# Another order for the jobs of an attention and gated convolution kernel

## The chip, the cores and the metric

The kernel runs on one core of a Trainium2 chip. The metric is the time of one execution on the device in microseconds (us), as the median of several runs. The engines are TensorE (PE in the profile, PEld its weight loads), VectorE (DVE), ScalarE (ACT), GpSimd (POOL) and SyncE (SP, which here only starts DMAs).

## The reference

```python
def _attn_ref(q, k, v):                    # (8, 8, 576, 64) each, float32
    ...                                    # rotary embedding of q and k by position
    scores = scale * np.matmul(q_rot, k_rot.transpose(0, 1, 3, 2))
    scores = scores - np.max(scores, axis=-1, keepdims=True)
    attn = np.exp(scores)
    attn = attn / (np.sum(attn, axis=-1, keepdims=True) + 1e-09)
    return np.matmul(attn, v)

def _moe_ref(x, w_val, conv_w, w_out):     # x: the 8 heads side by side, (8, 576, 512)
    ...                                    # xp: x with 4 rows of zeros in front
    for k in range(5):
        gate_pre += conv_w[k] * xp[:, k:k + S, :]
    gate = 1.0 / (1.0 + np.exp(-gate_pre))
    return gate * (x @ w_val) @ w_out
```

The two weight matrices and the convolution's taps arrive as 64-bit floats and are decoded on the chip.

## The kernel before

**Tiling.** The 64 heads are worked on as 32 pairs (p = 0 to 31), four pairs to a batch. A pair's q and k lie as 128 partitions (two heads of 64) by 576 positions. For a pair: the rotation is two multiplications and one addition each for q and k (`rope_mul`, `rope_add`; pair 0 adds on TensorE, `rope_mm`, with a matrix `swap` that ACT makes). Scores (`s_mm`) are computed for four blocks of 128 query rows by 576 keys and head, and for a fifth half block of both heads together (`s_mm` and `s_mix`). DVE takes the row maximum while it copies the scores to SBUF (`s_max`, line 428), ACT the exponential and its row sum (`s_exp`, line 436). TensorE transposes the result (`t_mm`, line 412), ACT or DVE copies it (`t_copy`), and TensorE multiplies with v (`pv_mm`, line 518, in four jobs for a pair, and `pv_left`, line 528, for the last 64 keys). The reciprocals of the row sums go through DRAM to be spread over the partitions (`r_write`, `r_read`), and `x_norm` multiplies with them. For pairs 0 to 6 (`WHOLE`) q and k stay in full precision; from pair 7 on they are split into a high and a low part (`qk_hi`, `qk_lo`), and a score is three products.

**The gated part.** Each pair's normalised x is one of four channel blocks of its batch. It is split into high and low (`x_hi`, `x_lo`); five taps make the gate (`tap`, `gate`); once all four pairs of a batch are there, two projections follow (`f_mm`, line 636: stage 0 with w_val, stage 1 with w_out, eight parts for each of four outputs), with `y_mul`, `y_hi`, `y_lo` between them and `o_out`, `o_dma` at the end. The weights are decoded in eight steps for each of eight blocks (`weight_step`), the taps in six (`tap_step`), both early in the kernel.

**Order.** Nothing is scheduled by a planner at run time. Functions add 3087 jobs to a list, with the engines that may do each and what it reads and writes. `ORDER` then says in which order they are issued: an entry is a job's number; V, A or G behind it chooses DVE, ACT or POOL where several may do it; the digits after a colon choose the buffers of the rings that the job opens (for TensorE one of four PSUM units); `<` names a job that this one is to wait for in addition. Every engine, and SP's DMA queue, works through its own entries in this order and waits, at each, for what its inputs and buffers need. `FILLS` puts 20 transpositions of the identity ahead of one entry.

**Numbers that come up.** 0: load of the taps, 1 to 6 their decoding; 7 and 8: the table's halves (on ACT's queue); 9: `tab_wrap`; 10: `make_swap`; 11, 16: loads of k of pair 0, 22, 31: of q; 27, 28: rotation multiplications of q's columns 0 to 256, 23, 24: 256 to 384, 32, 33: 384 to 640; 12, 13 and 17, 18: of k's halves; 14, 19, 25, 29, 34: `rope_mm`; 37: the first score job, 38 its maximum; 99 to 107 and 108 to 116: load and eight decoding steps of two blocks of w_val; 142, 143 and 141: rotation of q of pair 1; 136 to 139: of k of pair 1, with its wrap; 386: the first projection job; 2950 and 2955: the two transpositions of the last pair's sums (`r_mm`, line 550), 2949 and 2954 their reciprocals (`r_inv`); 2669 to 2672: four projection jobs of batch 6; 2933: a transposition of the last pair and 2934 its copy; 3047 to 3085: the last batch's outputs.

## Time and profile before

| | |
|---|---|
| runs | 620.99 us median of 3 (620.88 to 621.19) |
| profiled execution | 620.63 us, its span 618.8 us |
| TensorE busy | 609.4 us (98%), 8797 matmuls |
| DVE, ACT, POOL busy | 526.8 us (85%), 472.9 us (76%), 328.6 us (53%) |
| chain that ended last | PE 88%, DVE 6%, DMA 2%, ACT 2% |

A page of the profile tells of one execution. Busy shares are means over stages. In the chain of waits each piece is what the next one had waited for; its share says where the time passed that could not be overlapped. An engine's idle time costs something only where it stands on that chain. TensorE's records of matmuls overlap, so that a busy TensorE may still pass fewer matmuls than it could. L428 means line 428 of the kernel.

### The profile page before, as it was taken

The page shows a single profiled execution, that of the slowest core. Times are in us where ns is not written, and L with a number is a line of the kernel's source. Part 1 is how long each engine was busy: PE and PEld are TensorE (multiplying, and loading weights), DVE is VectorE, ACT ScalarE, POOL GpSimd, SP SyncE. Part 2 cuts the span into 40 slices and gives each one's busy share as a digit, 9 for nine tenths or more (in the row PEclk, how much of TensorE's full clock was granted, in tenths as well). Part 3 has the DMA queues.
Part 4 walks back from the last instruction along what each step waited for, and adds up shares of the span by engine and source line. Part 5 has one row for each costly group of instructions (what it writes and reads, how often), then busy time and mean ns, then how long its engine had stood idle before and what let it go on. Part 6 is the DMA issues. An engine that isn't in the chain of part 4 may idle for free.

```text
span 618.8 us, 21223 instructions
## 1 busy us (share of the span) xinstructions
PE 609.4 (98%) x8797; PEld 511.8 (83%) x8797; DVE 526.8 (85%) x1091; ACT 472.9 (76%) x993; POOL 328.6 (53%) x306
## 2 busy tenths in 40 slices
PE   8899999999999999999999999999999999999997
PEld 7566679888897979879898889788888889889697
DVE  6999999999998899998888888989888888777653
ACT  4999999999878887788887788766768775767421
POOL 2366444635445656466455457564454654688441
PEclk9999999999999999999999999999999999999999
DMA  8564631543524341435343234342333524201202
GB/s 252 171 200 149 197 115 58 155 138 119 158 68 147 100 137 64 139 118 158 117 140 119 81 119 137 116 140 64 96 119 100 177 62 149 90 20 52 71 21 77
DMA packets 42722, 72.85 MB, mean 118 GB/s; under 512 B 15449, under 2 KB 18050, under 8 KB 42626
## 3 DMA queue, kind: packets, MB, share of 16 engines
q1 hardware_dynamic: 41938, 70.74, 36.3%
q8 instruction: 69, 1.13, 0.8%
q10 hardware_dynamic: 688, 0.75, 0.4%
q14 instruction: 27, 0.22, 0.1%
HBM read 61.89 MB, written 9.59 MB: 115 GB/s over the span
## 4 chain that ended last, share of the span: by engine, by line
PE 88%; DVE 6%; DMA 2%; ACT 2%; issue 1%; SPq 0%; DVEq 0%; POOL 0%; POOLq 0%
PE ps_f L636 34%; PE ps_a L518 18%; PE ps_s L392 16%; PE ps_t L412 11%; PE ps_s L402 4%; PE ps_a L528 3%; DVE p L428 3%; ACT p L436 1%; ACT pt L505 1%; PE ps_s L412 1%; DMA wst<-in_w_val 1%; DVE qin L312 1%; DMA rb<-rd 1%; DMA tab<-in_tab 1%; DVE pm L428 0%
## 5 line engine op out<-in xcount | busy, mean ns | idle before, releaser
L436 ACT ACTIVATE p<-p,nm 128x576 f32<-128x576 f32 x256 | 197.3, 773 | 33.3 <-DVE p L428 32.1
L428 DVE TENSOR_SCALAR_CACHE_REDUCE p<-ps_s 128x576 f32<-128x576 f32 x256 | 184.1, 752 | 24.3 <-PE ps_s L392 21.4
L505 ACT COPY pt<-ps_t 128x1024 f32<-128x1024 f32 (+1 forms) x138 | 126.0, 929 | 23.8 <-PE ps_t L412 22.3
L392 PE MATMUL ps_s<-k,q 64*128 64x288 f32 x1424 | 137.5, 316 | 1.6 <-DVE q L318 0.5
L518 PE MATMUL ps_a<-pt,v 128*64 128x320 f32 (+1 forms) x1024 | 133.2, 410 | 0.1
L392 PEld LDWEIGHTS ps_s<-k,q 64*128 64x128 f32 x1424 | 111.5, 185 | 17.6 <-issue 4.0
L636 PE MATMUL ps_f<-y,wout_hi 64*128 64x288 f32 (+2 forms) x1024 | 109.0, 298 | 0.0
L518 PEld LDWEIGHTS ps_a<-pt,v 128*64 128x64 f32 x1024 | 69.9, 137 | 47.1 <-DVE p L428 1.1
L606 DVE SCALAR_TENSOR_TENSOR g<-x,cw,g 128x576 f32<-128x576 f32 (+2 forms) x113 | 93.3, 828 | 7.1 <-POOL g L604 3.6
L412 PEld LDWEIGHTS ps_t<-ident,p 64*128 64x128 f32 x2172 | 86.1, 139 | 10.3 <-issue 2.2
L412 PE MATMUL ps_t<-ident,p 64*128 64x64 f32 x2172 | 92.2, 223 | 0.4
L636 PEld LDWEIGHTS ps_f<-y,wout_hi 64*128 64x128 f32 x1024 | 87.1, 186 | 0.6 <-DVE x L577 0.2
L636 PE MATMUL ps_f<-xh,wval_hi 64*128 64x288 f32 (+2 forms) x512 | 84.8, 303 | 0.0
L636 PE MATMUL ps_f<-xl,wval_hi 64*128 64x288 f32 (+2 forms) x512 | 82.0, 292 | 0.0
L636 PE MATMUL ps_f<-xh,wval_lo 64*128 64x288 f32 (+2 forms) x512 | 82.0, 292 | 0.0
L636 PE MATMUL ps_f<-y,wout_lo 64*128 64x288 f32 (+2 forms) x512 | 81.7, 292 | 0.0
L312 POOL TENSOR_TENSOR kin<-kin,tab 128x576 f32<-128x576 f32 x41 | 58.3, 1428 | 37.5 <-DVE q L352 12.5
L312 POOL TENSOR_TENSOR qin<-qin,tab 128x640 f32<-128x640 f32 x32 | 50.0, 1566 | 36.1 <-DVE g L606 10.4
L636 PEld LDWEIGHTS ps_f<-xh,wval_hi 64*128 64x128 f32 x512 | 54.6, 185 | 0.8 <-issue 0.5
L636 PEld LDWEIGHTS ps_f<-xl,wval_hi 64*128 64x128 f32 x512 | 54.6, 185 | 0.1
L636 PEld LDWEIGHTS ps_f<-xh,wval_lo 64*128 64x128 f32 x512 | 54.6, 184 | 0.0
L636 PEld LDWEIGHTS ps_f<-y,wout_lo 64*128 64x128 f32 x512 | 54.5, 185 | 0.0
(135 smaller groups left out, 924.9 us busy)
## 6 DMA issues: line engine op xcount, KB each, us to landing
kin<-in_k SPq DMA_DIRECT2D x31, 576.0 KB
qin<-in_q SPq DMA_DIRECT2D x31, 512.0 KB
v<-in_v SPq DMA_DIRECT2D x32, 320.0 KB
out_t<-o SPq DMA_DIRECT2D x28, 288.0 KB
rb<-rd SPq DMA_DIRECT2D x31, 144.0 KB
rb<-rd SPq DMA_DIRECT2D x31, 128.0 KB
wst<-in_w_val SPq DMA_DIRECT2D x4, 512.0 KB
o<-in_w_out SPq DMA_DIRECT2D x4, 512.0 KB
```

The lines of the kernel that those rows point to most:

```text
L312: return eng.tensor_tensor(out=t[:, i, a:b], in0=t[:, 0 if p < RAW else i, a:b], in1=table[:, i, a:b], op=ALU.mult)
L392: T.matmul(out=tiles[h][:, half, 0:288], lhsT=operand(p, "q", h, x, c * 128, c * 128 + 128), rhs=operand(p, "k", h, y, k0 + half * 288, k0 ...
L402: inst = T.matmul(out=st["s8"][:, half], lhsT=operand(p, "q", h, x, 512, 640), rhs=operand(p, "k", h, y, D + half * 288, D + half * 288 + ...
L412: T.transpose(out=bank[0:src.shape[1], x, k * D:(k + 1) * D], in_=src[rows], identity=ident[rows, rows])
L428: return V.tensor_scalar(out=to, in0=st[f"s{i}"], scalar1=-SCALE if p in WHOLE else -1.0, scalar2=None, op0=ALU.mult, op1=ALU.min, accum_o ...
L436: return A.activation(out=to, in_=to if lifted else st[f"s{i}"], func=AF.Exp, bias=st[f"nm{i}"], scale=-1.0 if lifted else 1.0, accum_out= ...
L505: return A.copy(out=dst, in_=src)
L518: T.matmul(out=st[f"a{g}"][HEAD[h], 0:n], lhsT=st["v"][:, j, h, :], rhs=st[f"pt{g}"][:, h * 4 + j], start=(j == 0), stop=False)
L528: T.matmul(out=st[f"a{x}"][HEAD[h], 0:n], lhsT=st["v"][rows, 4, h, :], rhs=st["ptr"][rows, h, 0:n], start=False, stop=True)
L606: return eng.scalar_tensor_tensor(out=g, in0=x_sb, scalar=w, in1=g, op0=ALU.mult, op1=ALU.add)
L636: inst = T.matmul(out=acc[:, x, 0:hi - lo], lhsT=wt[w][HEAD[h], kc, dc * 128:(dc + 1) * 128], rhs=mv[HEAD[h], lo:hi], start=(turn == 0 and ...
```

## The change

The list of the order is replaced by another one, and the 20 filling transpositions move from entry 14 to entry 9. The jobs, their number and the buffers are the same; of the jobs that more than one engine may do, some change engine (DVE has 801 jobs for 792, ACT 697 for 702, POOL 277 for 281; TensorE 1101 and the DMA queue 211 as before). The decoding steps of taps and weights stand at other places too. Of the list, the head and the end are shown.

```diff
@@ -35,130 +35,130 @@
 LIFT = 0
 WHOLE = range(0, 7)
 ORDER = """
-7 22 11 8 16 0:0 10 31 9 27V 108 12V 28V 13V 29:0 17V 23V 24V 14:1 18V 30 99 32V 135 33V 25:2 15 144 1 19:3 2 3 26 4 109V 110V 34:0 111 20 21G 37:1
-114G 40:2 38:00 100A 140 46:3 112 35 43:1 47:11 39 101G 58:0 41:2 55:3 203 137G 44:3 42 48 36 45 59:20 52:2 136G 53:2 54 49:1 50:31 51 60 56:3 138V
-271 139V 141V 142V 143V 204V 67:0 61:2 68A:0 69:1 70A:0 71:3 72A 57 205G 62<68 63:2 5 6 150:01 153:01 77A:0 151:10 64 73:3 74A 154 65 102 66 145:21
-146:3 148:2 272G 208 160:03 78:2 152 75 80 82A:0 161:21 173:1 163:30 76A 81A 206G 149 147 174A:1 113 103 79A 209V 85:0 86 164 162 87 165:3 273V 181A:1
-105A 106G 210V 83:0 211V 155:12 104 207V 156:2 107G 348:100 349A 350G 157 158:3 159 88 89 171:1 166<181 274G 84 90 172A:1 91A:0 167:0 168 169 276 278G
-213:20 216:01 218:13 214:12 219:3 177:0 217 178A 175:2 182:1 221:0 117 179 170 184 176A 185A 180A 277V 279V 459 527 351 460G 183A 186A:1 215 222
...
-2920:20 2643<2877 2644 2645 2646 2924:23 2880 2927:2 2647A:1 2950:1 2951V:1 2923 2925:3 2926 2821G 2952:1 2928 2881:0 2882 2883 2884 2885 2921 2945:3
-2954 2955:1 2956A:0 2886 2658 2887G:0 2888G:1 2937:2 2938A 2933:0 2946V 2939:1 2940V 2935:3 2749V 2889G:2 2890V 2891V 2892V 2669:2 2670 2934A:1 2893V
-2671 2672 2943:0 2936A 2959:1 2960 2961 2962 2964 2944A 2963 2997:3 3011:0 2998 2999 2673<2944 2674 2675 2953 2965 2957:0 2958 2966 2676 2975G:2 2967G
-2968G:3 2977A:3 2983:1 2677A:0 2984 2985 2978G 2979V 2969A 3000 2970V 2976V 2986 3025:2 3026 3012 2894 3013 3001<2970 3002 3003 3014 3027 3028 2971G
-2980V 2981V 3004 3005 2987<2971 2988 2972V 2973V 2989 2990 3015<3005 3016 3017 3018 2822 2994 2995V 2750 2996V 2991 2992G 2993G 3022 2648 3006V 3007G
-2974 3008 3009A 3010V 3029<3005 3030 3031 3039:1 3032 3033 3034G 3040 3041 3042 3051:3 3052 3053 3054 3035G 2982 3036 3037A 3019 2678 3023V 3024V
-3020A 3021V 3043<3035 3044 3045 3063:2 3055<3021 3056 3057 3075:0 3076 3077 3038G 3078 3046 3049A:1 3050 3064 3065 3066 3058 3059V 3060 3079<3049 3080
-3081 3047V:0 3082 3067<3059 3068 3069 3070 3048 3061V 3062 3083V 3084 3085A 3086 3071V 3073V 3072 3074
+7 22 27V 28V 8 9 23V 11 10 29:0 24V 25:1 26 12V 13V 14:2 16 17V 18V 19:3 0:0 1 31 32V 33V 15 30 20 21A 108 109V 110V 111 112 34:1 99 100A 35 37:2
+38:00 39 114A 40:0 41:11 101G 102 43:3 42 44:2 45 58:2 46:1 47:3 48 52:0 53:20 54 135 136G 137G 140 49:3 138G 59:1 50:32 55:1 67:0 68A:0 69:2 51 139A
+36 56:3 142V 141V 143V 61:3 77A:0 71:1 62<77 113 203 271 63:0 70A:0 150:02 151:02 2 72A 60 64 204G 57 153:11 3 4 5 6 208 145:13 146:0 205G 65 272G
+75:0 76A 73:2 154 66 80 78 348:100 148:3 82V:0 74A 81A 79A 206V 160:13 152 149 103 161:21 162 105A 155:20 163:32 147 164 115G 87:1 88 156:3 157 85 86
+158:1 159 171:3 172A:1 165:2 181A:1 173:0 174A:1 349A 273G 89 104 209V 166<181 210V 83:0 459 84 211V 207A 461V 106V 116V 90 93A:0 213:30 144 107G
+167:0 218:12 274G 168 169 214:02 215 216:13 219:1 175:3 176A 217 182:0 170 179 183V 221:0 350G 177:1 178V 276 184 185A 180A 186V:1 223:32 226:22 220
...
+2917:0 2817A:3 2818V 2819G 2653<2861 2654 2655 2656 2874:1 2867:0 2871 2876 2869:3 2870V 2815A:2 2816G:4 2657A:0 2658 2868A 2872A 2875V 2639:2 2916
+2640 2641 2642 2878A:0 2877V 2919:03 2920:11 2643<2878 2644 2645 2922:33 2918 2646 2647V:0 2747V 2748G 2924:10 2943:3 2923 2925:2 2881:2 2944A 2883
+2882 2879:0 2884 2949 2927:0 2928 2880 2885 2926 2939:3 2749G 2886 2889G:2 2890G 2887G:4 2940V 2921 2950:1 2954 2937:0 2945:2 2951A:1 2888G:1 2669:1
+2670 2671 2952:1 2938A 2672 2955:3 2956V:0 2946A 2935:0 2936A:1 2933:2 2961:3 2962 2957:0 2934V 2959 2960 2963 2964 2673<2956 2674 2744G:3 2675 2997:0
+2891V 2953 2965 2648 2892G 2893V 2969A:1 2967V:0 2968G:2 2998 2676 2677A:0 2958 2966 2975V 2820V 2970V 2750 2983:2 2286 2984 2976V 2985 2986 3011:3
+3012 3013 3025:1 2678 2971V 2972V 2999 3026 3027 3000 3028 3014 2977A 2978V 2979V 2980V 2981V 2973G 2987<2971 2988 2989 2982 2974 2990 3001<2982 3002
+3003 3029<2974 2821V 2822 2994 2995A 3004 2894 3008 2991 3030 3031 3015<2974 3016 3032 3005 3017 3018 2996G 3009A 2992A 2993V 3006V 3007G 3010G 3033
+3034A 3019 3051:2 3052 3053 3054 3039:0 3020A 3021V 3022 3023A 3035V 3036 3037V 3040 3041 3042 3055<3022 3056 3057 3063:3 3024V 3064 3065 3075:1 3038V
+3066 3076 3077 3078 3058 3061A 3043<3024 3044 3062 3045 3067<3061 3068 3046 3069 3070 3079<3061 3080 3049A:1 3047V:0 3050 3081 3082 3083A 3085A 3048
+3059V 3060 3071V 3072 3073V 3074 3084 3086
 """
-FILLS = {14: (20, 0)}
+FILLS = {9: (20, 0)}
```

## Rows read from the trace of the kernel before

**Rows 1.** The page, busy us (share of the span) and instructions of each engine.
```profile
PE 609.4 (98%) x8797; PEld 511.8 (83%) x8797; DVE 526.8 (85%) x1091; ACT 472.9 (76%) x993; POOL 328.6 (53%) x306
```

**Rows 2.** Busy time by stage: PE, PEld, DVE, ACT, POOL (instructions), clock, DMA.
```profile
10.00:100.00 90.00, 86.67 (x1031) 61.85 (x1032) 87.40 (x192) 84.66 (x182) 44.94 (x42) 1.00 0.53 169
40.00:100.00 60.00, 59.42 (x730) 42.51 (x728) 59.00 (x125) 58.30 (x126) 29.96 (x27) 1.00 0.47 149
...
460.00:500.00 40.00, 40.00 (x620) 34.93 (x618) 33.36 (x65) 30.09 (x63) 22.04 (x22) 1.00 0.36 114
```

**Rows 3.** Instructions in order of time, first 12 us: start, us, engine, line [idle before].
```profile
6.47 0.30 ACT L763 COPY tab<-tab 128x128 f32<-128x128 f32 x1 [2.62 <-DMA tab<-in_tab]
...
6.85 0.61 DVE L312 TENSOR_TENSOR qin<-qin,tab 128x128 f32<-128x128 f32 x2
...
7.38 0.45 DVE L312 TENSOR_TENSOR kin<-kin,tab 128x288 f32<-128x288 f32 x1
...
9.99 1.25 PE L392 MATMUL ps_s<-k,q 64*128 64x288 f32 x8
...
10.33 0.69 DVE L703 SCALAR_TENSOR_TENSOR wst<-wst 128x512 int32<-128x512 int32 x1
...
11.26 0.76 DVE L428 TENSOR_SCALAR_CACHE_REDUCE p<-ps_s 128x576 f32<-128x576 f32 x1 [0.24 <-PE ps_s L392]
```

**Rows 4.** Groups by line, whole span: busy us, mean ns | idle before.
```profile
L606 DVE SCALAR_TENSOR_TENSOR g<-x,cw,g 128x576 f32<-128x576 f32 (+2 forms) x113 | 93.3, 828 | 7.1 <-POOL g L604 3.6 <-POOL g L610 1.2 <-PE ps_f L636 0.2
...
L312 POOL TENSOR_TENSOR qin<-qin,tab 128x640 f32<-128x640 f32 x32 | 50.0, 1566 | 36.1 <-DVE g L606 10.4 <-DVE qin L312 7.3 <-DVE kin L318 5.4
...
L312 DVE TENSOR_TENSOR qin<-qin,tab 128x640 f32<-128x640 f32 (+2 forms) x36 | 28.1, 792 | 3.4 <-DMA tab<-in_tab 2.9 <-DMA qin<-in_q 0.4
```

**Rows 5.** Chain of waits, 140 to 170 us: start, us, what.
```profile
141.97 2.13 PE ps_a L518 x16
144.11 0.99 PE ps_s L392 x12
...
145.59 2.09 PE ps_a L518 x16
...
157.05 0.80 PE ps_s L392 x12
...
161.00 4.04 PE ps_a L518 x32
```

**Rows 6.** Busy time by stage, 100 to 120 us, columns as above.
```profile
100.00:120.00 20.00, 19.91 (x281) 16.70 (x278) 19.33 (x42) 18.96 (x43) 10.62 (x9) 1.00 0.34 102
```

**Rows 7.** DVE's groups by line, 100 to 120 us.
```profile
L606 DVE SCALAR_TENSOR_TENSOR g<-x,cw,g 128x576 f32<-128x576 f32 x6 | 4.8, 805 | 0.1
...
L719 DVE TENSOR_TENSOR l<-l,wout_hi 128x512 f32<-128x512 f32 x1 | 0.7, 685 | 0.0
```

**Rows 8.** DVE and POOL in order of time, 45 to 51 us.
```profile
45.80 1.28 POOL L719 TENSOR_TENSOR l<-l,wout_hi 128x512 f32<-128x512 f32 x1 [1.13 <-ACT wout_hi L718]
...
46.68 0.95 DVE L719 TENSOR_TENSOR wst<-wst,wval_hi 128x512 f32<-128x512 f32 x1
...
48.29 0.68 DVE L720 TENSOR_TENSOR wval_lo<-wst 128x512 fp32r<-128x512 f32 x1
...
49.05 1.55 POOL L312 TENSOR_TENSOR qin<-qin,tab 128x640 f32<-128x640 f32 x1 [1.97 <-DVE wval_lo L720]
...
49.67 0.76 DVE L428 TENSOR_SCALAR_CACHE_REDUCE p<-ps_s 128x576 f32<-128x576 f32 x1
```

**Rows 9.** Instructions in order of time, last pair and end.
```profile
576.86 0.66 PE L473 MATMUL ps_t<-ident,p 128*128 128x128 f32 x4
577.99 0.28 PE L550 MATMUL ps_r<-ident,sums 128*9 128x128 f32 x1 [0.47 <-DVE sums L543]
...
613.73 0.44 ACT L677 ACTIVATE qin<-ps_f 128x320 f32<-128x320 f32 x1 [3.57 <-DVE qin L678]
...
614.97 0.89 DVE L678 TENSOR_SCALAR kin<-ps_f 128x320 f32<-128x320 f32 x2 [1.27 <-PE ps_f L636]
```

More of the change, by code (lines that the diff above doesn't have):

```diff
@@ new lines @@
+1127V 1312A 1315A 1316 1317A 1318A:1 1319:1 1320 1137 1307:0 1308A 1116A 1375:2 1104V 1105V 1258G 1259G 1376A:0 1369:1 1385V:0 1140:3 1141 1142 1143
+1370<1385 1359:02 1412V 1138V 1371:2 1360:21 1144<1138 1145 1146 1106 1372 1362:30 1363 1147 1148 1364:10 1367:3 1368 1361 1365:2 1366 1373 1421:23
+1149A 1150G 1377:0 1378A:0 1565G 1564G 1566G 1567G 1568G 1569G 1323:1 1572V 1573V 1574V 1422:00 1424:13 1139G 1321 1322 1423 1635 1128G 1324 1636G
+1413A 1374 1575 1325 1420 1426:20 1388:3 1642 1643G 1326 1329V:2 1427:1 1429:2 1425 1390A:0 1391:0 1392 1379:1 1380A 1383 1386 1387V 1381:2 1382A
@@ new lines @@
+1159A:0 1670<1685 1668 1677:3 1678A:1 1663 1675:2 1676A:1 1621:1 1623 1624 1671:0 1672 1713V 1719 1474V 1333V 1403V 1404V 1405V 1666 1406 1673 1674
+1622 1625 1726:03 1620 1626 1629A:3 1190 1786 1727:01 1728 1475G 1501:2 1502 1503 1688:1 1686 1504 1648 1720 1935 1687A 1689A 1729:13 1730 1787V
+1721:03 1722:0 1723 1724:2 1690V:1 1505<1689 1506 1507 1508 1681:0 1509 1683 1679:3 1725 1682A 1747:2 1748A:0 1684V 1788G 1789G 1790V 1791 1512:1 1513
+1514 1515 1680A 1731:02 1741:3 1476V 1477V 1478 1734:21 1732:33 1936G 1780V 1334 1757A:0 1516<1477 1517 1735 1518 1519 1742<1732 1520 1942 1743:0
@@ new lines @@
+2009V 2010V 2011V 1763:0 1816 1805 2079 1630V 1810 1817 1821:1 1767:2 1768 1499A 1500G 1765 1766 1769 1818 1764 1830:3 1827 1822A:1 1832 1833A 1770
+1771A:3 2014 2015G 1792 1834V:1 1835:1 1836 1819:0 1820A:1 1831V 1823:1 1824A 1828V 1702V 1703V 1523:2 1524 1525 1526 1949:30 1952:01 1950:12 1533:1
+2012G 2013G 1704V 1534 1535 1527<1952 1528 1529 1530 1536 1531A:1 1532 2016V 1954:03 1631V 1955:3 1825:2 1826A 2017V 2018G 1951 1537<1631 1538 1539
+1540 1953 1957:0 1959:02 1962:22 1960:31 1961 1839:3 1837 1838 1840 1627G:4 1628G:2 1958 1541A:1 1956 1773V:4 2080V 1542 1705V 1706 1841 1977:2
```

202 lines of the change are left out of this document (94 added, 108 removed).

## The prediction

> **What bounds the kernel now.** I read the page's busy shares first, then the busy time by stage, then the chain of waits. The shares name TensorE: it is busy 609.4 of 618.8 us, DVE 526.8, ACT 472.9 [rows 1]. By stages there are two regimes [rows 2]. From 40 to 100 us DVE is busy 59.0 of 60 us and ACT 58.3, and TensorE passes 12 matmuls per us: there it runs the slow full-precision matmuls of the first pairs, and DVE and ACT set the pace beside it. From 460 to 500 us TensorE is busy 40.00 of 40, with 15 matmuls per us, and DVE only 33.4. So an order can gain in three places: the head, up to about 100 us; the sequence of TensorE's own jobs after it; and the softmax of the last pair with the end. Nothing else is open, as the matmuls stay the same ones and the clock is granted in full (1.00) in every stage.
>
> **The start.** In the list before, DVE takes the multiplications of pair 0 in the order q, k, q, k, so that four of them need only the first half of the table; the second half lands at 6.47 us, where ACT copies its wrap [rows 3]. In the list after, the first q block (columns 0 to 256) is followed by the block 256 to 384, which needs the second half, and all four of k stand behind it. From the rows: 6.47, two of q (0.6), four of k at 0.45, ends at 8.9 us; before, the last of k began at 7.38 and ended at 7.8. Then a tap step (0.2), two of q (0.9) and four weight steps (2.0 by estimate: the third is the 0.69 of the row, the others about 0.43) give 11.9 us for the first maximum, against 11.26. TensorE is not later than that: its last two rotations take about 1 us each from 8.9, so its first score matmul moves from 9.99 to about 10.9 and ends before 11.9. ACT's wrap copy now stands ahead of the swap matrix, so the first rotation can't finish before about 7.2; this lies beside the multiplications of k. Three tap steps moved to later save DVE 0.5 by then and a fourth weight step costs 0.4, so at the same work done DVE is 0.7 us late. Bounds: 0 (the table lands earlier) to 1.4.
>
> **DVE's and ACT's lists in the head.** I counted what each list puts ahead of one TensorE job, the first scores of pair 5, before which both lists hold the same TensorE work. DVE loses four rotation multiplications, two rotation additions (0.8 each) and two wraps (0.2 each); it gets two taps (0.83), one lower part of x (0.7), two short weight steps (0.4), two long ones for one fewer (0.8), and two small copies (0.6): -5.2 + 4.7, or -0.5 us [rows 4]. ACT gets three wraps (0.3) and loses a weight step, a small copy and the copy of the reciprocals: -0.4. The rotations that DVE loses go to POOL, at 1.57 instead of 0.79. Ahead of the last PV job of pair 4 the same count gives -1.2 for DVE and +1.3 for ACT; I take the -0.5 on which the engines agree and keep -1.2 and +1.3 as the ends.
>
> **TensorE's sequence.** The PV matmuls use the array as 128 rows by 64 columns, nearly all else as 64 rows by 128. What going from one to the other costs is in the chain of waits [rows 5]: the 32 PV matmuls of a pair in one piece take 4.04 us, in two pieces 2.13 + 2.09, so 0.18 more; and the score job that follows a piece takes 0.99 instead of 0.80, so 0.19 more. An extra piece costs 0.37 us. The list before goes into PV 41 times, the list after 35: in the head (before the first projection) 10 against 6, after it 31 against 29. After the head this is on the path: 2 x 0.37, or -0.7 us. In the head, 4 x 0.37 = 1.5 us is TensorE's time, half hidden behind DVE: I take -0.7, with ends 0 and -1.5. Against this I counted how often, after the head, a PSUM unit is reopened with less than 1.2 us of TensorE work between its last matmul and the next occupant's first: 51 times before and 57 after. A maximum or a copy must fit in there. Six more at an estimated 0.2 us (a quarter of a 0.8 us operation) would be +1.2, which makes +0.5 the upper end here; I take nothing for it.
>
> **The last pair.** TensorE waits 0.47 us for the reciprocals ahead of its last transposition of sums [rows 9]. The list after puts four projection matmul jobs (1.6 us) in front of it, so this wait goes: -0.5. The end on the other side is +0.5, if what is late next (the copy, now DVE's, of the last transposed block) holds up the last PV. At the very end two outputs leave one after the other: 0.89 us on DVE before, 2 x 0.44 on ACT after. Nothing.
>
> **Sum.** +0.7 -0.5 -0.7 -0.7 -0.5 = -1.7 us on the profiled execution's 620.63 (618.8 of span and 1.8 around it), so 618.9; that execution lies 0.36 below the median of the runs, 620.99, and carried over to it the forecast is 619.3. The lower ends together give -3.9, the upper ones +3.7.
>
> **A rule against this change.** In the trace POOL and DVE take turns at one kind of work [rows 8]: a DVE subtraction of two SBUF tiles that began at 46.68, while POOL was in its operation of 45.80 to 47.08, took 0.95 us instead of 0.69 (the same operation in another stage [rows 7]), and POOL's multiplication began at 49.05, just after DVE's addition of two SBUF tiles had ended at 48.97, and is put down as waiting for it; the maximum at 49.67, which reads PSUM, ran inside POOL's operation at its usual 0.76. The Trainium skill (SBUF — State Buffer, Who interferes with whom) says the same in general: a DVE instruction with two SBUF inputs and a POOL instruction that reads SBUF lock each other out for a whole instruction. By that rule, which the trace bears out here, moving a rotation from DVE to POOL relieves nothing, since 1.57 us of the shared path takes the place of 0.79; with the -0.5 of DVE's list struck out the sum would be -1.2 us.
>
> **Rivals.** *A: the head's gaps close.* TensorE's idle time from 10 to 100 us, 90 - 86.67 = 3.3 us [rows 2], goes whole, because DVE's work ahead of the first projections no longer comes late. For it: both counts make DVE's list there lighter. Against: DVE is idle for 1.0 us in 60, so a list lighter by 0.5 can't give 3.3. Time: 620.99 - 3.3 - 0.7 - 0.5 = 616.5.
>
> *B: nothing to be measured.* The start's +0.7 eats the lists and half of the pieces, the wait for the reciprocals comes back as one for the last copy, and the tight reopenings take what the two pieces give: 620.4 to 621.5. For it: all terms are below 1 us, and each rests on a short stretch. That the change does nothing at all is excluded, since it also puts nine more jobs on DVE.
>
> *C: slower, by the path that POOL and DVE share.* Place: 100 to 140 us, where the first projections of batch 0 meet the rotations of the pairs behind them. From 100 to 120 us POOL is busy 10.62 of 20 us [rows 6], and DVE's operations on two SBUF tiles take 10.4 (eight kinds, from the 4.8 of the taps to the 0.7 of the subtraction [rows 7]): 21.0 of 20, so this path is full, counting the time in which one waits for the other. Up to the end of pair 6's PV the list after gives POOL three rotation additions and two multiplications more (5 x 1.57 = 7.8; the rest cancels), while DVE's two-tile work stays. Price: up to 7.5 us if all of it must be done by then; after pair 7 the two lists are level again, within 1.6 us, so part of it is only placed early; half is 3.7. Time: 619.3 + 3.7 = 623.0. It decides once a rotated q or k reaches TensorE after the job ahead of its scores has ended.
>
> **Chances.** About 0.2%, 1.24 us, is what a measurement of this kernel can tell from no change. Forecast 0.42 (its own range 617.6 to 619.7), A 0.13, B 0.25, C 0.20. So faster 0.55, same 0.25, slower 0.20. The range reaches below to A and a little of the lower ends, 615.6, and above to C at nearly half price, 622.8, which leaves most of C's dearer half and a corner of A out.
>
> **What would show it.** First score matmul near 10.9 us and first maximum near 11.9; 35 pieces of PV; no wait ahead of the last transposition of sums; DVE still busy for 59 of the 60 us from 40 to 100. Wrong: TensorE waiting for a rotated q or k between 100 and 140 us (C), its idle time from 10 to 100 us under 1 us (A), or new short waits for PSUM units after 140 us, which would void the gain of the sequence.

## The result and the profile after

The changed kernel takes 628.68 us in the median (626.61 to 629.62, 4 runs), the one before in the same comparison 621.09 (620.88 to 621.75, 4 runs): the ratio is 1.0116 [1.0089, 1.0142]. I had forecast 619.3, with 622.8 as the upper end. It is slower, by 7.6 us.

The profiled execution is the fastest of the four, 626.61 us with a span of 624.8, so 6.0 us more than in the profile before; its granted clock is 0.999 in the mean. The other three show 0.996 or 0.997 and 628.42 to 629.62. So some 6 us of the loss lie in the order itself. The other 1.6 I put down to the lower clock of those three (below); that is argued from the clocks and not shown.

The page's row of busy shares, to be set against [rows 1]:
```profile
PE 611.3 (98%) x8797; PEld 513.7 (82%) x8797; DVE 538.8 (86%) x1100; ACT 469.9 (75%) x988; POOL 336.9 (54%) x301
```

Busy time by stage: PE, PEld, DVE, ACT, POOL (instructions), clock, DMA share, GB/s; to be read beside [rows 2, 6]:
```profile
10.00:100.00 90.00, 85.50 (x987) 62.62 (x987) 86.56 (x190) 83.19 (x182) 46.51 (x40) 1.00 0.51 157
40.00:100.00 60.00, 59.24 (x719) 43.13 (x716) 58.30 (x127) 57.53 (x125) 31.83 (x28) 1.00 0.45 142
100.00:120.00 20.00, 19.94 (x304) 16.12 (x300) 19.57 (x43) 18.21 (x37) 12.32 (x11) 1.00 0.49 151
```
From 10 to 100 us TensorE is idle for 4.5 us instead of 3.3, and DVE is no busier than before: 58.3 of the 60 us from 40 to 100, for 59.0. At 100 to 120 us, where I had placed rival C, TensorE is idle for 0.06 us. From 460 to 500 it is busy 40.00 of 40, as before.

To see where the time went I compared the start of a TensorE job in both profiles, for jobs ahead of which both lists hold exactly the same TensorE jobs:

| | before | after | lost since the row above |
|---|---|---|---|
| first score matmul | 9.99 | 10.81 | +0.8 |
| last PV job of pair 4, just ahead of the first projection | 88.92 | 90.78 | +1.05 |
| a score job of pair 14, ahead of the next stage | 256.75 | 259.23 | +0.6 |
| one 20 us on | 276.59 | 281.46 | +2.4 |
| one 22 us on | 298.99 | 304.19 | +0.3 |
| end of the span | 618.8 | 624.8 | +0.8 |

So there are three places: the head, one stretch of some 40 us in the middle, where 2.7 us go, nearly all of it in the first 20, and the last 85 us (the difference is 5.20 at 299 us of the kernel before, 4.93 at 533 and 5.98 at the end); the 0.6 between 89 and 257 us is spread. Single profiles scatter by some tenths: where two kernels have the same entries, their profiles still drift apart by 0.95 us between 399 and 414 us (head_unlock and "after") and by 0.55 between 312 and 321 us (before_end and before).

**The start** went as worked out. Instructions in order of time (start, us, engine, line), to be read beside [rows 3]:
```profile
6.81 1.80 DVE L312 TENSOR_TENSOR kin<-kin,tab 128x288 f32<-128x288 f32 x4
...
10.81 2.60 PE L392 MATMUL ps_s<-k,q 64*128 64x288 f32 x13
...
12.08 0.76 DVE L428 TENSOR_SCALAR_CACHE_REDUCE p<-ps_s 128x576 f32<-128x576 f32 x1 [0.60 <-PE ps_s L392]
```
Four multiplications of k at 0.45 end at 8.6 us, the first scores begin at 10.81 and the first maximum at 12.08; forecast were 8.9, "about 10.9" and 11.9.

**The head.** Instructions in order of time, the idle time before one and its releaser in brackets:
```profile
24.16 0.73 DVE L708 SCALAR_TENSOR_TENSOR o<-o 128x20 int32<-128x20 int32 x1
...
25.24 1.40 POOL L312 TENSOR_TENSOR kin<-kin,tab 128x576 f32<-128x576 f32 x1
...
25.35 1.32 DVE L716 TENSOR_TENSOR cw<-o 128x20 f32<-128x20 f32 x1
...
27.27 0.20 DVE L545 RECIPROCAL pm<-sums 128x9 f32<-128x9 f32 x1
...
27.62 0.28 PE L412 MATMUL ps_t<-ident,pm 64*73 64x64 f32 x2 [2.52 <-DVE pm L545]
```
The order after puts four decoding steps of the taps, on 20 columns each, in front of pair 0's reciprocals (line 545) on DVE. Two of them met POOL. Line 708 took 0.73 us, where it took 0.18 in the list before. Line 716 began 0.11 us after a POOL multiplication and ended just behind it: 1.32 us for an operation that took 0.18 in the list before. The reciprocals come at 27.27, and TensorE, which needs them for its next transposition, stands still for 2.5 us.

**The middle.** The two stages that hold the loss, and then, of the kernel before, the stage with the same TensorE work as the second:
```profile
247.00:259.00 12.00, 11.95 (x213) 11.70 (x212) 11.73 (x22) 9.96 (x20) 2.64 (x4) 1.00 0.21 66
259.00:291.00 32.00, 29.92 (x437) 23.82 (x436) 28.37 (x57) 24.85 (x52) 29.30 (x25) 1.00 0.35 102
```
```profile
257.00:287.00 30.00, 29.96 (x444) 24.12 (x442) 27.15 (x60) 26.55 (x57) 18.38 (x18) 1.00 0.41 124
```
Before, TensorE is busy 29.96 of 30 us; after, 29.92 of 32. POOL has 29.3 us of work there instead of 18.4, while it had been idle for most of the 12 us ahead. In order of time, the same stage:
```profile
261.61 1.62 DVE L312 TENSOR_TENSOR qin<-qin,tab 128x640 f32<-128x640 f32 x1
...
263.33 1.18 DVE L318 TENSOR_TENSOR qin<-qin 128x640 f32<-128x640 f32 x1
...
263.93 1.85 POOL L604 TENSOR_TENSOR g<-term,g 128x576 f32<-128x576 f32 x1
264.55 1.58 DVE L345 TENSOR_SCALAR q<-qin 128x640 fp32r<-128x640 f32 x1
...
266.90 0.77 ACT L436 ACTIVATE p<-p,nm 128x576 f32<-128x576 f32 x1 [2.00 <-DVE p L428]
...
267.67 0.28 ACT L363 CAST k<-k 128x128 fp32r<-128x128 f32 x1
...
268.01 1.06 PE L392 MATMUL ps_s<-k,q 64*128 64x288 f32 x12 [1.39 <-ACT k L363]
```
The chain from q's rotation to its high part (lines 312, 318, 345: 0.82, 0.82 and 0.49 us where POOL leaves them alone) took 1.62, 1.18 and 1.58, beside two taps that POOL works on at that moment (lines 603 and 604). Two maxima stand behind it on DVE. ACT waits 2.00 us for the first of them, and the wrap of pair 15's k (line 363), which stands on ACT behind that maximum's exponential, is done 1.39 us after TensorE could have begun the scores that need it. Over the whole span I counted the DVE operations that took more than 0.25 us beyond the usual time of their line and width: 14 before, 8.9 us too long together, and 23 after, 12.9 us; between 255 and 275 us none before and four after, 2.5 us.

**The end.** Around the last pair's reciprocals, beside [rows 9]:
```profile
583.60 0.71 PE L412 MATMUL ps_t<-ident,p 64*128 64x64 f32 x16 [0.43 <-ACT p L436]
584.35 0.28 PE L550 MATMUL ps_r<-ident,sums 128*9 128x128 f32 x1
```
The wait ahead of the transposition of sums (line 550) is gone, and an ordinary transposition just ahead of it waits 0.43 us instead.

**The pieces of PV** are 35, as counted, but no gain is to be seen beside them. Chain of waits, to be read beside [rows 5], and then the score job of its first line in order of time:
```profile
144.91 1.23 PE ps_s L392 x12
```
```profile
143.72 1.43 POOL L355 TENSOR_TENSOR k<-kin,k 128x576 fp32r<-128x576 f32 x1
...
145.20 0.70 PEld L392 LDWEIGHTS ps_s<-k,q 64*128 64x128 f32 x10 [0.17 <-POOL k L355]
```
The score job ahead of the merged piece takes 1.23 us, not 0.80: from its third matmul on it needs the low part of pair 9's k, which POOL (line 355) has ready only at 145.15. That is the sign that I gave for rival C, TensorE waiting for a rotated k, 5 us behind the stretch that I named and for some 0.4 us.

### The profile page after: what moved, and what is told of

Read it like the earlier page. It is cut to its first block, busy times and chain, and to the rows that moved or that the text cites. A ratio compares the mean times of both kernels' runs of the same rounds, so it can differ in the third digit from the quotient of the medians.

```text
span 624.8 us, 21247 instructions
## 1 busy us (share of the span) xinstructions
PE 611.3 (98%) x8797; PEld 513.7 (82%) x8797; DVE 538.8 (86%) x1100; ACT 469.9 (75%) x988; POOL 336.9 (54%) x301
## 4 chain that ended last, share of the span: by engine, by line
PE 82%; DVE 10%; ACT 3%; issue 3%; POOL 1%; DMA 1%; ACTq 0%; DVEq 0%; POOLq 0%
PE ps_f L636 30%; PE ps_a L518 18%; PE ps_s L392 16%; PE ps_t L412 11%; PE ps_s L402 4%; DVE p L428 3%; PE ps_a L528 3%; DVE g L606 1%; ACT pt L505 1%; ACT p L436 1%; DVE qin L312 1%; DMA tab<-in_tab 1%; PE ps_r L327 1%; PE ps_s L412 1%; DVE g L649 1%
## 5 line engine op out<-in xcount | busy, mean ns | idle before, releaser
L392 PEld LDWEIGHTS ps_s<-k,q 64*128 64x128 f32 x1424 | 114.3, 185 | 15.6 <-issue 4.2
L636 PE MATMUL ps_f<-y,wout_lo 64*128 64x288 f32 (+2 forms) x512 | 84.7, 292 | 0.0
L636 PE MATMUL ps_f<-xh,wval_hi 64*128 64x288 f32 (+2 forms) x512 | 82.0, 302 | 0.0
L312 POOL TENSOR_TENSOR qin<-qin,tab 128x640 f32<-128x640 f32 x40 | 62.8, 1577 | 32.4 <-DVE g L606 11.8
L636 PE MATMUL ps_f<-xl,wval_hi 64*128 64x288 f32 (+2 forms) x512 | 79.4, 292 | 0.0
L636 PE MATMUL ps_f<-xh,wval_lo 64*128 64x288 f32 (+2 forms) x512 | 79.3, 292 | 0.0
L636 PEld LDWEIGHTS ps_f<-y,wout_lo 64*128 64x128 f32 x512 | 58.4, 185 | 0.0
L636 PEld LDWEIGHTS ps_f<-xh,wval_hi 64*128 64x128 f32 x512 | 51.9, 185 | 0.4 <-DVE p L428 0.2
L636 PEld LDWEIGHTS ps_f<-xl,wval_hi 64*128 64x128 f32 x512 | 51.9, 185 | 0.1
L636 PEld LDWEIGHTS ps_f<-xh,wval_lo 64*128 64x128 f32 x512 | 51.9, 185 | 0.0
```

The costliest lines, as they stand in the source:

```text
L312: return eng.tensor_tensor(out=t[:, i, a:b], in0=t[:, 0 if p < RAW else i, a:b], in1=table[:, i, a:b], op=ALU.mult)
L392: T.matmul(out=tiles[h][:, half, 0:288], lhsT=operand(p, "q", h, x, c * 128, c * 128 + 128), rhs=operand(p, "k", h, y, k0 + half * 288, k0 ...
L636: inst = T.matmul(out=acc[:, x, 0:hi - lo], lhsT=wt[w][HEAD[h], kc, dc * 128:(dc + 1) * 128], rhs=mv[HEAD[h], lo:hi], start=(turn == 0 and ...
```

## The experiments

All are this kernel with another list, and nearly all are "after" with a few entries moved. The ratio is always against the kernel before, measured beside it. Where a loss is given at a place, it is the difference between the starts of equal TensorE jobs, from the profiled executions.

One thing must be added to what stands above on the order. The kernel's `run` makes each POOL job of eleven kinds (rotation, splits, wraps, taps, weight steps) wait, beside its inputs and buffers, for the DVE job of these kinds that stands last ahead of it in the list. So an edit that moves such a job can also change what a POOL job waits for.

### The head

My first theory was the taps' steps ahead of the reciprocals; its rival, that POOL's multiplication beside line 716 is what costs, wherever the steps stand.

```diff
-153:11 3 4 5 6 208 ... 82V:0 74A          taps_later
+153:11 208 ... 82V:0 3 4 5 6 74A
```


> The list after, with the four tap steps 3 to 6 moved from in front of DVE's reciprocals of pair 0 to behind them. In the list after, TensorE stands still from 24.6 to 27.6 us for these reciprocals. Theory L (DVE's small steps stood locked out by POOL's rotation multiplication: the last tap step took 1.32 us beside POOL's 1.40): the reciprocals come at about 25.3 instead of 27.27 us, the wait falls by about 2.2 us and stays away, as DVE also loses the 1.7 us of locked time: span 622.4 to 623.0 instead of 624.8. If the pause is also what lowers the granted clock to 0.996 to 0.997 in three of four runs, the clock comes back to 1.000 and the median falls from 628.7 to about 624.6. Rival O (DVE's list is simply late there and paces the head): the wait comes back before 100 us, first projection still at 92.5 us, the time stays at 627 to 629. Rival S (the loss is spread over small PSUM waits in the body): same as O in the total.

Measured: 629.04 us, 1.0128 [1.0109, 1.0147]. At 27.6 us it was 1.8 us ahead of "after" (2.1 gained), and by 32.5 us 2.7 behind it: the load of w_out's block (348) shares a buffer with the taps and now stood ahead of their last steps, so that DVE waited 2.10 us for that DMA (and the taps are decoded from an overwritten buffer, here and in three_places). The first half agrees with the theory; the second was my mistake in the edit.

```diff
-65 272G 75:0 ... 115G 87:1                head_unlock
+65 75:0 ... 115G 272G 87:1
```


> The list after with one job of POOL moved: its first multiplication of pair 3's k goes behind the weight step that follows it in POOL's list, so that POOL is idle while DVE does its last tap step and the reciprocals of pair 0; DVE's list is untouched. Theory L: the last tap step falls from 1.32 to about 0.2 us, the reciprocals come at about 26.2 instead of 27.27, TensorE's wait at 24.6 to 27.6 us shrinks by 1.1 us, time 1.1 us below the list after (profiled span about 623.7). Rival O (position in DVE's list alone): nothing there changes, 27.3 us, same time as the list after.

Measured: 627.83, 1.0105 [1.0091, 1.0119]. In order of time:
```profile
25.76 0.18 DVE L716 TENSOR_TENSOR cw<-o 128x20 f32<-128x20 f32 x1
...
26.90 0.28 PE L412 MATMUL ps_t<-ident,pm 64*73 64x64 f32 x2 [1.38 <-ACT pt L505]
...
30.02 2.80 POOL L312 TENSOR_TENSOR kin<-kin,tab 128x576 f32<-128x576 f32 x2
...
31.45 1.92 DVE L713 SCALAR_TENSOR_TENSOR wst<-wst 128x512 f32<-128x512 uint32 x1
```
Without the multiplication beside it, line 716 takes 0.18 us and TensorE waits 1.1 us less. But the POOL operation must be done somewhere: from 30.02 on line 713 on DVE, 0.7 us elsewhere, takes 1.92 beside it, and by 43 us the kernel is 0.4 us behind "after". So the rival is right about a part of the mechanism, 1.1 us of the wait, and taking the neighbour away only moves the meeting.

```diff
-153:11 3 4 5 6 208 ... 78 348:100 148:3 82V:0 74A     recip_first
+153:11 208 ... 78 148:3 82V:0 3 4 5 6 348:100 74A
```


> The list after, with the tap steps 3 to 6 behind the copy of pair 0's reciprocals in DVE's list, and the load of w_out's second block, which uses the taps' buffer, behind them (its first decoding step starts at 37.2 us, so it has time). Theory: TensorE's 2.6 us pause at 24.6 to 27.6 us shrinks to about 0.5; as the DMA stall of the earlier try at this place (2.1 us on DVE) can't come, the matmuls are 1.5 to 2.2 us earlier at the first projection, the clock falls in fewer of the runs, and the median goes from 628.7 to 625 to 626. Rival (DVE's list paces the head whatever stands first): the wait comes back before 92 us, and the median is above 627.5.

Measured: 626.10 (625.03 to 626.56, 5 runs), 1.0076 [1.0063, 1.0088]. In order of time:
```profile
25.26 0.21 DVE L545 RECIPROCAL pm<-sums 128x9 f32<-128x9 f32 x1 [0.26 <-POOL sums L536]
...
25.62 0.28 PE L412 MATMUL ps_t<-ident,pm 64*73 64x64 f32 x2 [0.44 <-ACT p L436]
```
```profile
29.25 2.10 PE L518 MATMUL ps_a<-pt,v 128*64 128x320 f32 x14 [0.90 <-DVE p L428]
```
The reciprocals come 2.0 us earlier, the transposition too, and the wait ahead of it falls from 2.52 to 0.44; of these 2.1 us head_unlock took 1.1 by removing the meeting alone, and the rest is the place of the steps. Then 1.0 us is given back by 30 us, where the PV job waits for a maximum that stands behind the moved steps. What is left is 0.97 us, at the last PV job of pair 4 as at 250 us. So the reciprocals explain nearly the whole loss of the head beyond the start (0.97 of 1.05). The spans differ by 1.6; the other 0.6 comes up between 256 and 297 us, where the two lists are the same. The median gains 2.6, and the clock is 0.999 or 1.000 in all five runs, where three of four of "after" had 0.996 or 0.997; that the rest of the median is clock is argued from this.

```diff
-63:2 5 6 150:01 ... 66 145:21             before_plus: the kernel before, with
+63:2 150:01 ... 66 5 6 145:21             this and the edit of before_end
```


> The same with the tap steps 5 and 6 behind the reciprocals of pair 0. In the trace of the kernel before, tap step 5's first operation took 0.99 us beside POOL's 1.42 instead of 0.18, and TensorE then waited 0.5 us for a maximum. Theory L: another 0.5 to 0.8 less at 24 us, of which DVE keeps part: 619.9 to 620.4. Rival (DVE paces the head whatever stands first): as without it, 620.5.

Measured: 622.97, 1.0032 [1.0021, 1.0043]. In order of time:
```profile
25.18 1.41 POOL L312 TENSOR_TENSOR kin<-kin,tab 128x576 f32<-128x576 f32 x1 [0.89 <-DMA qin<-in_q]
25.24 1.38 DVE L716 TENSOR_TENSOR cw<-o 128x20 f32<-128x20 f32 x1
```
The last tap step, moved from one place to another in the good list, falls in with the same POOL operation and takes 1.38 us for its 20 columns; 0.8 us gained at 21 to 25 us, 1.5 lost at 25 to 26. The effect belongs to the meeting, not to either list: the list before has one too, line 713 at 22.22 us, 0.99 for 0.18, but with nothing behind it that TensorE waits for as long.

### Halves of one list and the other

Jobs of the same set can be put in the order of either list; the seam has to be judged by the trace.

```diff
 ...        b434_a:  first 434 jobs of "after" in the order of before, the rest as after
 ...        a434_b:  first 434 jobs of before in the order of after, the rest as before
 ...        b1500_a, a1500_b, b2685_a: the same with 1500 and 2685 jobs
```


> The opposite splice: the first 434 jobs as in the list before, then the rest of the list after. Theory H: 621.0 + 2.5 + 1.3 = 624.8; with the pause at 24.6 us gone the clock falls in fewer runs, so the scatter is below 1 us. Rival W: 621. Rival P (the fewer pieces of PV in the rest of the list after do save 0.7 us, and the trace's loss there is the head's carried on): 620 to 620.5.

> A splice: the first 434 jobs of the list before (up to about 85 us), in the order and on the engines of the list after; then the rest of the list before, word for word but for the numbers of the buffers. By the traces, at the first projection the kernel after is 2.35 us late (92.49 against 90.14). Theory H (each stretch costs what the traces show at equal work: head +2.4, 85 to 293 us +2.5, the rest +1.3): 623.0 to 623.6, and in the runs in which TensorE's pause at 24.6 to 27.6 us lowers the granted clock for 3.4 us, 1.7 more, so a median of 623 to 625. Rival D (the head's delay is slack that the list before has room for later): 621.0 to 621.6. Rival W (the whole loss is the head's, the rest only carries it): 627 to 629.

Measured: b434_a 625.84, 1.0080 [1.0066, 1.0093], in the profile 1.7 us less than "after". a434_b 627.99, 1.0112 [1.0098, 1.0126], but 4.5 us of its loss stand at the seam, 80 to 96 us, with a stretch of low clock, so that it says little of the head. The first agrees with the table: with the head of before, and so also with its start, the kernel is 1.9 us ahead of "after" at the end of the head and 1.7 at the end of the span, and more than 4 us lie behind it.

> The first 1500 jobs as in the list before, the rest from the list after. Theory H: 621.0 + 1.3 = 622.3. Rival T (most is lost after 293 us, in small waits for PSUM units and in the last pair): above 624. If the rest of the list after is the better one: 620.5 or less.

> The first 1500 jobs (to about 293 us) in the order and on the engines of the list after, the rest from the list before. Theory H: 621.0 + 2.4 + 2.5 = 625.9, with the clock's falls 626 to 628. Rival W: the same as the splice at 434 jobs. Rival T (most is lost in the rest): under 624.5.

> The first 2685 jobs (to about 526 us) as in the list before, then the end of the list after. The splice at 1500 jobs lost 1.3 us, in the trace from 510 us on. If the end loses it (a maximum and the reciprocals of the last pair late on DVE): 622.0 to 622.4. If it is lost between 293 and 526 us: 620.5 to 621.2.

Measured: b1500_a 622.23 (11 runs), 1.0016 [1.0008, 1.0025]; a1500_b 635.43, 1.0228 [1.0208, 1.0247], with 7.6 us lost at its seam near 300 us and a fall of the clock there, and another in the head, not usable; b2685_a 624.76, 1.0058 [1.0045, 1.0072], with a loss of 3.0 us at its seam (531 to 543 us) and 0.2 to 0.3 lost in the part that was to be tested (in it a block of batch 5's output is overwritten before it is sent). b1500_a is the one that counts. Its stage is:
```profile
257.00:287.00 30.00, 29.96 (x445) 24.11 (x443) 25.01 (x57) 26.34 (x56) 16.87 (x17) 1.00 0.43 126
```
With the first 1500 jobs in the order of before, the stage is full again (29.96 of 30), as it must be where the list is that of before. What the run adds is the other half: the kernel is 0.2 us ahead of before at 299 us, 0.1 behind at 524, and at no place between more than 0.6 away. So the loss up to 292 us is made by the arrangement of the first 1500 jobs, and the new list behind them, with its pieces of PV, neither gains nor loses more than 0.3 until about 520 us. From there to the end it loses 1.1; "after" loses as much there (1.05 behind 533 us), 0.7 of it by the time that TensorE is at 545 us of the kernel before.

### The stage from 256 to 292 us

Theory: the two taps (1258, 1259) beside the rotation of pair 16's q. Rival: POOL has too much in this stage, and the meeting moves.

```diff
-1105V 1258G 1259G 1376A:0 ... 1569G 1323:1           pair_unlock
+1105V 1376A:0 ... 1569G 1258G 1259G 1323:1
```


> The list after with two taps of pair 12 on POOL (1258, 1259) moved behind the wrap of pair 16's k in POOL's list, so that POOL doesn't use SBUF's shared path while DVE rotates pair 16's q at 261.6 to 266 us; DVE's list is untouched. Theory L: DVE's three operations there fall from 1.62, 1.18 and 1.58 us to about 0.8, 0.8 and 0.5, the maxima of pair 15 come 2.2 us earlier, and TensorE's waits at 266.6 (1.4 us) and 270.2 (0.5) go: time 2.0 to 2.5 us below the list after, about 626.4 against 628.7 in the median if the clock stays as it was. Rival O: DVE's operations stay as long as they were, no gain (0 to 0.3). Rival S: the waits go but come back within the next 30 us as others.

Measured: 631.89, 1.0169 [1.0155, 1.0183]. In order of time, and then its head by stages of 1 us (columns as above):
```profile
263.08 0.82 DVE L312 TENSOR_TENSOR qin<-qin,tab 128x640 f32<-128x640 f32 x1
...
264.87 0.49 DVE L345 TENSOR_SCALAR q<-qin 128x640 fp32r<-128x640 f32 x1
...
266.93 3.39 POOL L312 TENSOR_TENSOR kin<-kin,tab 128x576 f32<-128x576 f32 x2
...
269.00 1.63 DVE L611 TENSOR_SCALAR g<-x,cw 128x576 f32<-128x576 f32 x1
...
271.36 0.72 PE L412 MATMUL ps_t<-ident,p 64*128 64x64 f32 x16 [1.27 <-DVE p L428]
```
```profile
26.00:27.00 1.00, 0.00 (x0) 0.00 (x0) 1.00 (x2) 0.54 (x1) 0.75 (x1) 1.00 0.00 0
...
30.00:31.00 1.00, 1.00 (x7) 1.00 (x5) 0.55 (x1) 0.81 (x3) 1.00 (x1) 0.50 0.75 94
```
The three DVE operations are at 0.82, 0.82 and 0.49 again and the first wait is gone, 1.5 us. Then line 611, 0.83 in "after", takes 1.63 beside POOL's multiplications of k, TensorE waits 1.27 us, and by 288 us 3.8 are lost: 0.7 at that wait, 1.1 beside a second stretch of low clock (granted 0.70, 0.50, 0.50 and 0.59 in the four stages of 1 us from 273 us on), and 2.0 where TensorE waits for POOL's part of y:
```profile
287.21 0.40 PE L636 MATMUL ps_f<-y,wout_hi 64*128 64x288 f32 x2 [1.77 <-POOL y L664]
```
The head's rows show the clock: after TensorE has stood still at 26 to 27 us, it is granted 0.50, that is 1.2 GHz, up to about 31 us. This kernel's head is that of "after" to the entry; that stretch cost 1.2 us against the profile of "after", which has the same pause (2.52 us) and no low clock.

three_places made this edit, that of taps_later and one at the end (2927 ahead of 2949) at once:

> The list after with three edits together: the tap steps behind the reciprocals of pair 0, POOL's two taps of pair 12 behind the wrap of pair 16's k, and the reciprocals of the last pair's first sums behind the maximum that follows them in DVE's list (there DVE's 2-column addition took 1.38 us beside POOL's 1.41). Theory L with these three places as the cause: 2.2 + 2.3 + 0.6 less, profiled span about 619.7, clock 1.000, median 621 to 622, level with the kernel before. Rival S (loss spread over the body): at least 625. If the cause is elsewhere in the head: 624 to 626.

Measured: 631.47, 1.0166 [1.0145, 1.0188]. The gains don't add up, and the taps' mistake is in it too; nothing follows for the parts.

```diff
-... 1573V 1574V 1422:00 1424:13 1139G ... 1374 1575 1325      pair_order: DVE's q chain
-... 1326 1329V:2 1427:1 1429:2 1425                           behind the scores' maxima
+1323:1 1422:00 1424:13 1572V 1573V 1139G ... 1374 1325
+1388:3 1427:1 1429:2 1574V 1575 1642 1643G 1326 ... 1329V:2 1425
```


> The list after with DVE's four jobs on pair 16's q (1572 to 1575) and a tap (1329) moved behind the maxima of pair 15's next two blocks, and the load and the first multiplication of pair 17's q moved with them. If the 2.8 us that are lost from 256 to 272 us are DVE's place in the list, lengthened by POOL: TensorE's waits at 266.6 and 270.2 go, and no buffer or result is late that they need: 2 to 2.8 us less than the list after, median 626 to 626.5. If the loss is POOL's (the parts of y and pair 16's k come late whatever DVE does): less than 0.7 us, as when POOL's taps were moved.

Measured: 631.45, 1.0167 [1.0153, 1.0181]. In order of time:
```profile
271.18 1.93 DVE L352 SCALAR_TENSOR_TENSOR q<-qin,q 128x640 fp32r<-128x640 f32 x1
...
275.22 1.56 PE L392 MATMUL ps_s<-k,q 64*128 64x288 f32 x10 [3.23 <-DVE pt L507]
```
The first waits are gone; line 352 met POOL instead, the copies behind it came late, TensorE stood still for 3.2 us, and a stretch of low clock followed. A chain of q that is put off is as dear as one that is stretched.

```diff
-1105V 1258G 1259G 1376A:0 ... 1326 1329V:2          recip_pair: recip_first, the taps
+1105V 1376A:0 ... 1326 1329A:2 ... 1117G 1258G 1259G  far behind, one copy on ACT
```


> The list after with the reciprocals of pair 0 ahead of the tap steps (the edit that gave 626.1), and at the stage of pair 15 two edits: POOL's two taps of pair 12 behind its last part of y of batch 2 (in the earlier try they stood in front of it, and TensorE waited 2 us for it at 285 us), and pair 13's first tap on ACT instead of DVE, where POOL had stretched it to 1.63 us. Theory L (what is lost from 256 to 273 us is DVE's time beside POOL's 10 us of added work in this stage): the waits at 266 and 270 us go, nothing of y is late, 2 to 2.8 us less than 626.1: 623.3 to 624.1, granted clock 1.000. Rival (the stage is full on DVE whatever POOL does): 625.5 to 626.5.

> The same with the first 38 jobs (up to the first score job) in the order and on the engines of the list before. By the traces the start costs 1.1 to 1.4 us at equal work. If that is carried through the head: 1.1 to 1.4 us less than the kernel with the first two edits. If DVE takes it back later in the head: less than 0.5.

Measured: recip_pair 628.44, 1.0121 [1.0106, 1.0135]; recip_pair_start, the same with the first 38 jobs as before, 627.45, 1.0103 [1.0090, 1.0117]. recip_pair's instructions in order of time:
```profile
285.39 0.20 POOL L536 TENSOR_SCALAR sums<-sums 128x9 f32<-128x9 f32 x1
285.62 0.22 DVE L545 RECIPROCAL pm<-sums 128x9 f32<-128x9 f32 x1 [1.10 <-POOL sums L536]
...
285.89 0.28 PE L412 MATMUL ps_t<-ident,pm 64*73 64x64 f32 x2 [0.82 <-DVE pm L545]
```
The stage gained 0.8; then the sums of pair 15 (line 536), queued on POOL behind the two taps, came late, DVE waited 1.10 us for them and TensorE 0.82: 3.4 us went between 283 and 289. The two spans differ by 0.85 us, but that isn't the start: it gives 0.16 (first scores at 10.79 us, for 10.95), and the rest comes up at 70 to 72 and 400 to 410 us, where both lists are the same. As the start of before came late in this profile, neither of the two outcomes that I had expected is tested by it.

```diff
-1105V 1258G 1259G 1376A:0                 pool_idle: recip_first, the taps in the
+1136 1258G 1259G 1571G                    12 us in which POOL was idle
```


> The list after with the reciprocals of pair 0 ahead of the tap steps (626.1), and POOL's two taps of pair 12 moved the other way: in front of its first multiplication of pair 16's q, where POOL stands idle for 7 to 8 us because that q hasn't landed (250 to 258 us). So 4.3 us leave the stage from 259 to 291 us, in which POOL is busy 29.3 of 32 us, and nothing is put behind anything. Theory L (the 2.8 us lost from 256 to 273 us come from POOL's added work in that stage, by the path it shares with DVE and by its own lateness): 1.4 to 2.8 us less than 626.1, 623.3 to 624.7, POOL about 25 of 32 us there. Rival (the taps lock DVE as long wherever they stand; the wait comes forward to 253 to 258 us): 625.5 to 626.5.

> The same move in the splice that has the list before up to 434 jobs and then the list after (625.84). Theory L: 1.4 to 2.8 us less, 623.0 to 624.4. Rival: 625.3 to 626.3.

Measured: pool_idle 627.22 (625.90 to 629.24), 1.0099 [1.0082, 1.0116]; b434_pool_idle, the same edit on b434_a, 628.73, 1.0112 [1.0099, 1.0125]. pool_idle by stage, and in order of time:
```profile
257.00:289.00 32.00, 30.05 (x440) 24.12 (x440) 28.81 (x62) 23.74 (x51) 22.58 (x19) 1.00 0.31 89
```
```profile
253.25 1.59 POOL L604 TENSOR_TENSOR g<-term,g 128x576 f32<-128x576 f32 x1
...
254.13 2.54 DVE L606 SCALAR_TENSOR_TENSOR g<-x,cw,g 128x576 f32<-128x576 f32 x2
...
257.06 0.67 PE L402 MATMUL ps_s<-k,q 64*128 64x288 f32 x6 [0.88 <-DVE pr L507]
```
POOL's work in the stage falls from 29.3 to 22.6 us, and the wait at 268 us shrinks by 1.2, of which 0.8 comes back 1.6 us on. But in their new place the taps on POOL meet two taps on DVE (line 606: 2.54 for two, 0.83 each elsewhere), TensorE waits 0.88 at 257, and 1.5 us are lost at 255 to 257. In b434_pool_idle the same place costs 4.3 us (254 to 258), with waits of 0.74 and 1.80 us and a stretch of low clock behind them (0.50 up to 262 us). The surplus is cheaper in no place that I tried.

### Two steps of the prediction by themselves

```diff
+2945:3 2669 2670 2671 2672 2954 ... 2934A        before_end: before, four projection jobs
-... 2669:2 2670 2934A:1 2893V 2671 2672          ahead of the transposition of sums
```


> The list before with one edit: the four projection jobs 2669 to 2672 go in front of the last transposition of sums, as in the list after (buffers of the transpositions around them changed so that all are free). By the prediction's term: 0.5 less, 620.5. If the copies or the last PV are late instead: 621.0 or more.

Measured: 621.85 (11 runs), 1.0009 [1.0000, 1.0018]. The wait of 0.47 us went, 0.46 gained at 577 us, and 0.25 and 0.72 came back as waits for the copies: the other end that the prediction gives for this step (+0.5; by the starts +0.45). That wait had a cause of its own. DVE and POOL in the kernel before:
```profile
576.04 1.40 POOL L604 TENSOR_TENSOR g<-term,g 128x576 f32<-128x576 f32 x1
576.10 1.36 DVE L542 TENSOR_SCALAR sums<-sums 128x3 f32<-128x3 f32 x1 [2.45 <-ACT p L436]
```
Three columns on DVE took 1.36 us, where the next two took 0.14: beside POOL's tap again.

```diff
-... 880 877 ... 934A:1 931:3 932A:1 922          pv_split: before, 12 PV blocks cut in two
+... 880 931:3 932A:1 877 ... 934A:1 922          (one of 12)
```


> The list before with twelve PV blocks after 160 us cut in two: the transposition ahead of each block goes in between its second and third job (its copy behind it). By the prediction's 0.37 us for a piece: 12 x 0.37 = 4.4, so 625.4. If a piece costs only what the matmuls of the block itself show (4.04 against 2.13 + 2.09): 12 x 0.18 = 2.2, 623.2. If it costs nothing on the path: 621.0 to 621.3.

Measured: 633.27, 1.0193 [1.0179, 1.0207], that is 11.9 us over the kernel before in the same comparison, or 0.99 for each cut. One of them in order of time:
```profile
330.34 1.95 PE L518 MATMUL ps_a<-pt,v 128*64 128x256 f32 x16
...
332.22 0.71 PE L412 MATMUL ps_t<-ident,p 64*128 64x64 f32 x16
...
332.86 2.38 PE L518 MATMUL ps_a<-pt,v 128*64 128x320 f32 x16
```
From the first PV matmul to the job behind the last (335.17) the cut block with its transposition takes 4.83 us; in the kernel before the same transposition and the same block, one after the other, take 4.62 (325.15 to 329.77), 0.21 less. Over the twelve cuts the PV matmuls by themselves take 4.18 us for 4.03, and in the nine blocks that hold no wait the difference with the transposition is 0.07 to 0.21, in the median 0.19. So the turn costs some 0.2 us, not the 0.37 that I read from [rows 5]. The rest of the 0.99 is for the greater part waiting: TensorE is idle for 7.2 us between 155 and 525 us, for 0.1 before, and 3.3 of them, in three of the cuts, are waits for a copy (line 505). A list moved in twelve places loses that much.

## Why the prediction was wrong

- **The start** (+0.7): right. Eleven kernels with the new start have their first scores at 10.95 us in the median (10.7 to 11.2), nine with the old one at 10.28 (9.9 to 10.9): +0.67.
- **DVE's and ACT's lists in the head** (-0.5): the step that failed first. I summed durations up to a TensorE job at the far end and took a lighter list for an earlier one. What decided was which entries stand ahead of pair 0's reciprocals, and that two of them met POOL: TensorE waits 2.52 us for these reciprocals. Measured for the head with its PV pieces: +1.05 (1.87 at the last PV job of pair 4 less the 0.82 of the start), where I had -1.2; recip_first takes back 0.97 of it. So the -0.7 for the head's pieces isn't to be seen either.
- **TensorE's sequence** (-0.7 after the head): the term that failed by most. The count of 31 against 29 pieces holds, the price of a turn doesn't: some 0.2 us in pv_split for 0.37, since the 0.99 of [rows 5] was the dearest of seven such score jobs (0.89 to 0.99). So two pieces are worth 0.4 us, not 0.7, and no profile shows even that; b1500_a, with the new list from 293 us on, is level up to 520. In place of a gain one stage gave +2.7: there POOL's work had grown from 18.4 to 29.3 us, DVE's steps for q were stretched beside it, and TensorE waited for k's wrap behind them. The term had nothing for DVE operations that don't keep their usual time, and no stage by stage count of POOL. For the six more tight reopenings I had taken nothing; what they cost isn't shown.
- **The last pair** (-0.5): the wait went and came back, as before_end shows; this was the other end. The loss of the last 85 us, 1.05 in "after" and 1.1 in b1500_a, has come up for the most part before the last pair's sums: 0.9 of it by 557 us of the kernel before.
- **The rule against this change** was the right page read too narrowly. I struck out the -0.5 and stopped, when [rows 8] showed DVE operations that are stretched. The Trainium skill (SBUF — State Buffer, Who interferes with whom) also says that copies, casts and single-input scalar operations in the two-port modes contend, and that the order of issue decides who blocks. The trace agrees: line 345, one SBUF input, took 1.58 us for 0.49. One of the two pieces of evidence that I gave for the rule was none: POOL's multiplication at 49.05 us waited for DVE's addition because `run` makes it wait for the last weight step ahead of it in the list. The stretched subtraction at 46.68 stands.
- **Rival C** had the mechanism and not the place. From 100 to 140 us nothing happened; just behind it, at 145 us, TensorE waited some 0.4 us for a low part of k, and the surplus on POOL came at 257 to 299 us, with 2.7 us lost, where I had put 3.7. I judged one stage by its share and didn't go through the others, and read POOL's surplus from a sum ("after pair 7 the two lists are level again") instead of by stages.
- **The clock** I had at 1.00 throughout. Five profiles have the head of "after" with its pause of TensorE of 2.5 us; in three of them (pair_unlock, pair_order, a1500_b) a stretch at 1.2 GHz follows, in two ("after", a434_b) none.

In the profiled execution the sum reads: +0.8 start, +1.05 head, +0.6 from 89 to 257 us, +2.7 from 257 to 299 us, +0.8 from there to the end, 6.0 in all; the forecast was -1.7.

**Open.** That the stage's loss lies in the arrangement of the first 1500 jobs is shown, and that POOL's operations stretch DVE's there is read from the rows. Whether POOL's 11 us more or the exact meetings make the 2.7 us isn't settled: each of the four moves took away its wait and made another. Nor is it shown in which runs of "after" the clock falls in the head; that is taken from the three profiles named and from recip_first's clocks. The 1.1 us at the end of b1500_a, and the 0.6 between 89 and 257 us, were not tracked down, and no list that I ran beats the one before.

## What to carry to other kernels

Before a list of durations is summed, look for what stands directly ahead of the one entry that the busiest engine waits for, and at what the engine sharing its path does at that moment: operations of 20 columns can cost what their neighbour still has to do. When work moves to a second engine, make the balance by stages, since a total that is level may be 11 us too much in one stage of 32. And where a wait is taken away, follow the entry that made it: nearly every edit here that took one away made another, mostly within 10 us.
